# First cross layer: the opening row products of a half-unit's first tile move into the row block of the half-unit before

## The chip, the cores and the metric

One core of a Trainium2 chip runs the whole kernel. The metric is the device time in microseconds (us); the kernel before takes 131.48 us, the median of 3 runs (131.47 to 131.52).

## The reference, cut to what matters

Six cross layers on 4096 rows of 416 features, in bf16:

```python
B, F, D, L = 4096, 26, 16, 6          # Din = 416
def reference(x0, ws, bs):            # x0 (4096, 416), ws (6, 416, 416), bs (6, 416)
    x = x0
    for l in range(ws.shape[0]):
        x = x0 * (x @ ws[l] + bs[l]) + x
    return x
```

## The kernel before

**Layout.** The features lie on the partitions. 416 = 3 x 128 + 32: three blocks of 128 features (index m for outputs, k for inputs) and a remainder of 32. Columns are the 4096 batch rows: two units (s) of 2048 columns, each of four groups (g) of 512. `XM[i]` holds the three full blocks; `XR[i]` holds the remainder, with the four column groups of a unit stacked on partitions 0, 32, 64 and 96, so that one tile of 512 columns holds the remainder of a whole unit. `XRd` is a copy of the first remainder with its halves exchanged, so that group g also stands 64 partitions away. `WM`, `WR` and `WD` hold the weights: full rows, the 32 remainder rows repeated on all four partition groups, and a block form for the remainder's outputs.

**Products.** For an output block m, 512 columns get three full products (128 input rows each, L208 in the first layer, L173 in 32-column strips in the middle layers, L304 in the last) and one row product, which adds the 32 remainder rows. A row product uses only 32 rows of the array, at row group 0, 32, 64 or 96. Row products are at L226 in the first layer, at L179 (`mm_row`) in the middle layers and at L310 in the last. The remainder's outputs come from `mm_rem` (L185, L190).

**Behind the products.** `ew_main` takes a finished tile of 128 x 1024: ACT adds the bias and casts to bf16 (L159), DVE multiplies by x0 (L160) and adds x (L161). `ew_rem` does the same for the remainder (L165 to L167). All tiles that TensorE writes come from one pool, `psum`, of four buffers with one tag (`"ps"`); a tile waits until a buffer is free, that is until all that used the tile before it are done.

**First layer.** `first_layer(s)` runs once for each unit. It goes over two half-units h of two column groups each (gl = 0, 1). A half-unit takes three tiles `ph0` to `ph2`, one for each m, does 18 full products into them, and then one block of six row products in the order m = 0, 1, 2. The row group is `32 * ((2 * h + gl) ^ (2 if m == 1 else 0))`: for h = 0 it is 0, 32 (m = 0), 64, 96 (m = 1, from `XRd`), 0, 32 (m = 2); for h = 1 it is 64, 96, then 0, 32, then 64, 96. In h = 1 the tile `pr` follows, with `mm_rem` in its first half and, for s = 0, the transposes of unit 1's remainder (`x0_rem(1)`, L151) in its second half; DVE copies these into `XR[0]` and `XRd` (L154). For s = 0 and h = 0, `x0_rem(0)` does the same for unit 0 between the two column groups, with the tile `tpr` of its own.

**Middle layers and the end.** Layers 1 to 4 go over pairs of tiles (s, m); for the second tile of a pair the row products stand first and open the sums, right behind the first tile's row products: eight in a block. The last layer works with batch rows on the partitions, in four rounds, and stores the output.

**Order.** The instructions of each engine run in one fixed order. It follows the program's order in the main, but where an instruction's inputs come late, a later one that is ready may be laid ahead of it, on DVE above all.

Of the kernel before, what the change touches and what calls it, by code (L numbers as in the profile page):

```python
# [11 lines left out]
BF16 = mybir.dt.bfloat16  # L12
FP32 = mybir.dt.float32
# [3 lines left out]
def kernel(  # L17
# [7 lines left out]
    nc = tc.nc  # L25
    B, D = x0.shape
    L = ws.shape[0]
    P = 128
    NK = 3
# [4 lines left out]
    CW = 512  # L34
# [8 lines left out]
    psum = ctx.enter_context(tc.tile_pool(name="psum", bufs=4, space=bass.MemoryType.PSUM))  # L43
# [8 lines left out]
    WM = const.tile([P, L, NK, D], BF16)  # L52
    WR = const.tile([P, L, D], BF16)
# [10 lines left out]
    XRd = big.tile([P, NS * CW], BF16)  # L64
# [3 lines left out]
    def col0(s, g):  # L68
        return SW * s + CW * g
# [79 lines left out]
    def x0_rem(s, tpr):  # L149
        for i in range(4):  # L150
            nc.tensor.transpose(tpr[:, 128 * i:128 * i + 128], xrig[:, s, i, :], ident[:])  # L151
        for dst, src in ((slice(0, P), slice(0, P)), (slice(64, P), slice(0, 64)), (slice(0, 64), slice(64, P))):
            to = XR[0] if dst == src else XRd
            nc.vector.tensor_copy(to[dst, CW * s:CW * s + CW], tpr[src])  # L154

    def ew_main(l, s, m, h, pt, cur, nxt):
        c0 = col0(s, 2 * h)
        t = tpool.tile([P, 2 * CW], BF16, name="t")
        nc.scalar.activation(t[:], pt[:].rearrange("p a b -> p (a b)"), ACT.Identity, bias=bM[:, m, l:l + 1], scale=1.0)  # L159
        nc.vector.tensor_tensor(out=t[:], in0=t[:], in1=XM[0][:, m, c0:c0 + 2 * CW], op=ALU.mult)  # L160
        nc.vector.tensor_tensor(out=nxt[:, m, c0:c0 + 2 * CW], in0=t[:], in1=cur[:, m, c0:c0 + 2 * CW], op=ALU.add)  # L161

    def ew_rem(l, s, pr, curR, nxtR):
        tr = tpool.tile([P, 2 * CW], BF16, name="t")
        nc.scalar.activation(tr[:, 0:CW], pr, ACT.Identity, bias=bR[:, l:l + 1], scale=1.0)  # L165
        nc.vector.tensor_tensor(out=tr[:, 0:CW], in0=tr[:, 0:CW], in1=XR[0][:, CW * s:CW * s + CW], op=ALU.mult)  # L166
        nc.vector.tensor_tensor(out=nxtR[:, CW * s:CW * s + CW], in0=tr[:, 0:CW], in1=curR[:, CW * s:CW * s + CW], op=ALU.add)  # L167
# [15 lines left out]
    def mm_rem(l, s, pr, cur, curR):  # L183
        for g in range(NG):
            nc.tensor.matmul(pr[32 * g:32 * g + 32, :], lhsT=WD[:, l, g, :], rhs=curR[:, CW * s:CW * s + CW],  # L185
                             start=True, stop=False, tile_position=(0, 32 * g))
        for k in range(NK):
            for g in range(NG):
                c0 = col0(s, g)
                nc.tensor.matmul(pr[32 * g:32 * g + 32, :], lhsT=WM[:, l, k, NK * P:D], rhs=cur[:, k, c0:c0 + CW],  # L190
                      start=False, stop=(k == NK - 1), tile_position=(0, 32 * g))
# [7 lines left out]

    def first_layer(s):  # L200
        cur, curR, nxt, nxtR = XM[0], XR[0], XM[1], XR[1]
        for h in range(2):
            pt = [psum.tile([P, 2, CW], FP32, tag="ps", name=f"ph{m}") for m in range(NK)]

            def full(m, gl):
                c0 = col0(s, 2 * h + gl)
                for k in range(NK):
                    nc.tensor.matmul(pt[m][:, gl, :], lhsT=WM[:, 0, k, 128 * m:128 * m + 128], rhs=cur[:, k, c0:c0 + CW],  # L208
                                     start=(k == 0), stop=False)

            if s == 0 and h == 0:
                for gl in range(2):
                    for m in range(NK):
                        full(m, gl)
                    if gl == 0:
                        tp0 = psum.tile([P, CW], BF16, tag="ps", name="tpr")
                        x0_rem(0, tp0[:])
            else:
                for m in range(NK):
                    for gl in range(2):  # L220
                        full(m, gl)
            for m in range(NK):
                for gl in range(2):
                    rg = 32 * ((2 * h + gl) ^ (2 if m == 1 else 0))
                    src = XRd if m == 1 else curR
                    nc.tensor.matmul(pt[m][:, gl, :], lhsT=WR[rg:rg + 32, 0, 128 * m:128 * m + 128],  # L226
                                     rhs=src[rg:rg + 32, CW * s:CW * s + CW],
                                     start=False, stop=True, tile_position=(rg, 0))
            if h == 1:
                pr = psum.tile([P, 2, CW], FP32, tag="ps", name="pr")  # L230
                mm_rem(0, s, pr[:, 0, :], cur, curR)
                if s == 0:
                    x0_rem(1, pr[:, 1, :].bitcast(BF16)[:, 0:CW])
            for m in range(NK):
                ew_main(0, s, m, h, pt[m], cur, nxt)
            if h == 1:
                ew_rem(0, s, pr[:, 0, :], curR, nxtR)

    bias_setup()
    pe_filler(1, CW)  # L240
    for s in range(NS):
        first_layer(s)
# [15 lines left out]
    cur, curR = XM[1], XR[1]  # L258
    for l in range(1, LL):
        nxt, nxtR = XM[1 + (l % 2)], XR[1 + (l % 2)]  # L260
# [29 lines left out]
        cur, curR = nxt, nxtR  # L290
# [99 lines left out]
```

## Time and profile before

| | |
|---|---|
| median of 3 runs | 131.48 us (131.47 to 131.52) |
| profiled execution | 131.97 us |
| its span | 130.1 us |
| PE busy | 124.2 us (95%) |
| DVE busy | 107.5 us (83%) |
| ACT busy | 85.8 us (66%) |
| granted TensorE clock | 0.999 |

The span runs from the first to the last instruction of the profiled execution; 1.87 us lie around it. PE is TensorE's matmuls and PEld its weight loads, which overlap the matmuls. DVE is VectorE, ACT ScalarE. The chain is the work that ended last, followed back from the last instruction. Names such as L226 are lines of the kernel before.

### The profile page before, as it was taken

The numbers are of one execution on the slowest core, as the hardware profiler recorded it, in microseconds if no ns is written. First come the engines' busy times: TensorE is split into PE (matmuls) and PEld (weight loads), VectorE is DVE, ScalarE is ACT, GpSimd is POOL, SyncE is SP. The second block draws the span as 40 slices with busy tenths as digits, with TensorE's granted clock in tenths as the row PEclk, the third lists the DMA queues.
The fourth block names the chain that finished last, engine by engine and source line by source line (L and its number), as shares of the span: only waits on it lengthen the run. The fifth ranks groups of instructions, "written<-read, shape, count | busy, mean of one in ns | idle before, by whom it ended". The sixth has DMA issues, their size and how long they took to land.

```text
span 130.1 us, 3968 instructions
## 1 busy us (share of the span) xinstructions
PE 124.2 (95%) x1688; PEld 55.2 (42%) x1690; DVE 107.5 (83%) x197; ACT 85.8 (66%) x97; POOL 5.8 (4%) x17
## 2 busy tenths in 40 slices
PE   6999999999999999999999999999999999999960
PEld 2343343444444444545444434444445445445420
DVE  1012989999998898999898989898989899898991
ACT  0044594788849485849486849577848896569670
POOL 4002110610000000000000000000000000000000
PEclk9999999999999999999999999999999999999999
DMA  3999999999990000000000000000197999995754
GB/s 102 211 219 225 149 198 242 243 327 333 333 306 12 5 0 3 5 0 5 0 5 0 5 0 5 0 0 5 30 176 162 121 220 180 195 306 191 234 170 132
DMA packets 42185, 16.45 MB, mean 126 GB/s; under 512 B 30894, under 2 KB 42168, under 8 KB 42168
## 3 DMA queue, kind: packets, MB, share of 16 engines
q1 hardware_dynamic: 39368, 15.53, 54.4%
q10 hardware_dynamic: 2800, 0.67, 2.8%
q8 instruction: 13, 0.21, 0.7%
q14 instruction: 4, 0.03, 0.1%
HBM read 6.23 MB, written 3.41 MB: 74 GB/s over the span
## 4 chain that ended last, share of the span: by engine, by line
PE 89%; DVE 6%; issue 2%; ACT 1%; DVEq 0%
PE pt L173 49%; PE ph L208 13%; PE py L304 8%; PE pt L179 5%; PE pr L190 5%; DVE t L332 3%; PE wps L135 3%; DVE o L321 2%; PE pr L185 2%; PE ph L226 2%; PE py L310 1%; PE py L313 1%; ACT t L331 1%; PE tpr L151 0%; PE pr L151 0%
## 5 line engine op out<-in xcount | busy, mean ns | idle before, releaser
L173 PE MATMUL pt<-XM,WM 128*32 128x512 bf16 x1152 | 65.2, 379 | 0.0
L159 ACT ACTIVATE t<-pt,bM 128x1024 bf16<-128x1024 f32 x48 | 49.6, 1115 | 17.6 <-PE pt L179 17.6
L160 DVE TENSOR_TENSOR t<-t,XM 128x1024 bf16<-128x1024 bf16 x60 | 41.3, 690 | 6.0 <-ACT t L159 6.0
L161 DVE TENSOR_TENSOR XM<-t,XM 128x1024 bf16<-128x1024 bf16 x60 | 41.7, 696 | 3.4
L173 PEld LDWEIGHTS <-WM 128*32 128x32 bf16 x1152 | 29.8, 97 | 33.9 <-issue 5.4
L331 ACT CAST t<-py 128x416 bf16<-128x416 f32 (+1 forms) x23 | 14.8, 642 | 4.8 <-PE py L304 2.6
L304 PE MATMUL py<-WM,XM 128*128 128x416 bf16 x96 | 17.7, 340 | 0.0
L159 ACT ACTIVATE t<-ph,bM 128x1024 bf16<-128x1024 f32 x12 | 12.5, 1112 | 7.5 <-PE ph L226 7.5
L208 PE MATMUL ph<-XM,WM 128*128 128x512 bf16 x70 | 16.9, 387 | 0.2
L304 PEld LDWEIGHTS <-XM 128*128 128x128 bf16 x96 | 9.0, 98 | 8.5 <-issue 1.4
L332 DVE TENSOR_TENSOR t<-t,X0rows 128x416 bf16<-128x416 bf16 (+1 forms) x23 | 10.4, 456 | 1.2 <-ACT t L331 1.2
L208 PEld LDWEIGHTS <-WM 128*128 128x128 bf16 x72 | 6.9, 99 | 8.9 <-issue 1.9
L321 DVE TENSOR_TENSOR o<-t,XLrows 128x416 bf16<-128x416 bf16 (+1 forms) x23 | 10.4, 455 | 0.0
L165 ACT ACTIVATE t<-pr,bR 128x512 bf16<-128x512 f32 x10 | 6.4, 685 | 3.0 <-PE pr L190 2.1
L190 PE MATMUL pr<-XM,WM 128*32 128x512 bf16 x120 | 8.2, 379 | 0.0
L179 PE MATMUL pt<-XR,WR 32*128 32x512 bf16 x96 | 7.3, 379 | 0.0
L106 ACT ACT_TABLE_LOAD x1 | 1.3, 1283 | 6.6 <-DMA XM<-in_x_dram 6.6
L135 PE MATMUL wps<-warm 128*128 128x512 bf16 (+1 forms) x11 | 4.4, 593 | 1.2 <-DVE warm L94 1.2
L167 DVE TENSOR_TENSOR XR<-t,XR 128x512 bf16<-128x512 bf16 x10 | 4.2, 425 | 0.7
L190 PEld LDWEIGHTS <-WM 128*32 128x32 bf16 x120 | 3.2, 97 | 3.0
L166 DVE TENSOR_TENSOR t<-t,XR 128x512 bf16<-128x512 bf16 x10 | 4.2, 418 | 0.0
L125 POOL COPY WD<-WR 32x32 bf16<-32x32 bf16 (+1 forms) x8 | 3.4, 424 | 16.6 <-DMA WR<-in_ws_dram 16.3
(37 smaller groups left out, 29.7 us busy)
## 6 DMA issues: line engine op xcount, KB each, us to landing
X0rows<-in_x_dram SPq DMA_DIRECT2D x4, 832.0 KB, 11.6
out_dram<-o SPq DMA_DIRECT2D x9, 208.0 KB, 2.5
WM<-in_ws_dram SPq DMA_DIRECT2D x5, 312.0 KB
out_dram<-o SPq DMA_DIRECT2D x13, 104.0 KB, 1.8
WR<-in_ws_dram SPq DMA_DIRECT2D x4, 130.0 KB, 4.1
WM<-in_ws_dram ACTq DMA_DIRECT2D x1, 312.0 KB
XM<-in_x_dram SPq DMA_TRANSPOSE x8, 5.8
xrig<-in_x_dram ACTq DMA_DIRECT2D x4, 32.0 KB, 4.5
```

What stands on the lines that cost most here:

```text
L135: nc.tensor.matmul(wps[:, 0:cols], lhsT=warm[:, 0:P], rhs=warm[:, 0:cols], start=True, stop=True)
L159: nc.scalar.activation(t[:], pt[:].rearrange("p a b -> p (a b)"), ACT.Identity, bias=bM[:, m, l:l + 1], scale=1.0)
L160: nc.vector.tensor_tensor(out=t[:], in0=t[:], in1=XM[0][:, m, c0:c0 + 2 * CW], op=ALU.mult)
L161: nc.vector.tensor_tensor(out=nxt[:, m, c0:c0 + 2 * CW], in0=t[:], in1=cur[:, m, c0:c0 + 2 * CW], op=ALU.add)
L173: nc.tensor.matmul(pts[g // 2][32 * q:32 * q + 32, g % 2, :], lhsT=WM[:, l, k, 128 * m + 32 * q:128 * m + 32 * q + 32], rhs=cur[:, k, c0:c ...
L179: nc.tensor.matmul(pts[g // 2][:, g % 2, :], lhsT=WR[32 * g:32 * g + 32, l, 128 * m:128 * m + 128], rhs=curR[32 * g:32 * g + 32, CW * s:CW ...
L190: nc.tensor.matmul(pr[32 * g:32 * g + 32, :], lhsT=WM[:, l, k, NK * P:D], rhs=cur[:, k, c0:c0 + CW], start=False, stop=(k == NK - 1), tile ...
L208: nc.tensor.matmul(pt[m][:, gl, :], lhsT=WM[:, 0, k, 128 * m:128 * m + 128], rhs=cur[:, k, c0:c0 + CW], start=(k == 0), stop=False)
L304: nc.tensor.matmul(py[:, 0:D], lhsT=cur[:, k, q_cols(q, g)], rhs=WM[:, l, k, :], start=((not closes) and k == 0), stop=(closes and k == NK ...
L321: tc.keep_in_program_order(nc.vector.tensor_tensor(out=o, in0=t, in1=xl, op=ALU.add))
L331: nc.scalar.copy(tv, src)
L332: tc.keep_in_program_order(nc.vector.tensor_tensor(out=tv, in0=tv, in1=X0rows[:, b, :], op=ALU.mult))
```

## The change

In both units, the two row products of h = 1's tile `ph0` (m = 0) move from the end of h = 1 into the row block of h = 0 and open that tile's sum. The block of h = 0 now holds eight row products, in the order `ph0` of h = 0, `ph0` of h = 1, m = 2, m = 1 (row groups 0, 32, 64, 96, 0, 32, 64, 96). The block at the end of h = 1 holds four (m = 1 and m = 2; row groups 0, 32, 64, 96). h = 1's `ph0` is closed by its last full product (`stop`), and it takes its buffer ahead of h = 0's row block.

```diff
-        for h in range(2):
-            pt = [psum.tile([P, 2, CW], FP32, tag="ps", name=f"ph{m}") for m in range(NK)]
...
+        def full(pt, m, h, gl, after_row):
+            c0 = col0(s, 2 * h + gl)
+            for k in range(NK):
+                nc.tensor.matmul(pt[:, gl, :], lhsT=WM[:, 0, k, 128 * m:128 * m + 128], rhs=cur[:, k, c0:c0 + CW],
+                                 start=(k == 0 and not after_row), stop=(k == NK - 1 and after_row))
+
+        def row(pt, m, h, opens):
+            for gl in range(2):
+                rg = 32 * ((2 * h + gl) ^ (2 if m == 1 else 0))
+                src = XRd if m == 1 else curR
+                nc.tensor.matmul(pt[:, gl, :], lhsT=WR[rg:rg + 32, 0, 128 * m:128 * m + 128],
+                                 rhs=src[rg:rg + 32, CW * s:CW * s + CW],
+                                 start=opens, stop=not opens, tile_position=(rg, 0))
+
+        def ph(m):
+            return psum.tile([P, 2, CW], FP32, tag="ps", name=f"ph{m}")
+
+        pa = [ph(m) for m in range(NK)]
...
+        pb = [ph(0)]
+        row(pa[0], 0, 0, False)
+        row(pb[0], 0, 1, True)
+        row(pa[2], 2, 0, False)
+        row(pa[1], 1, 0, False)
+        for m in range(NK):
+            ew_main(0, s, m, 0, pa[m], cur, nxt)
+        for m in range(NK):
+            if m:
+                pb.append(ph(m))
+            for gl in range(2):
+                full(pb[m], m, 1, gl, m == 0)
+        row(pb[1], 1, 1, False)
+        row(pb[2], 2, 1, False)
+        pr = psum.tile([P, 2, CW], FP32, tag="ps", name="pr")
+        mm_rem(0, s, pr[:, 0, :], cur, curR)
+        if s == 0:
+            x0_rem(1, pr[:, 1, :].bitcast(BF16)[:, 0:CW])
+        for m in range(NK):
+            ew_main(0, s, m, 1, pb[m], cur, nxt)
+        ew_rem(0, s, pr[:, 0, :], curR, nxtR)
```

More of the change, by code (lines that the diff above doesn't have):

```diff
@@ L201, in first_layer @@
         cur, curR, nxt, nxtR = XM[0], XR[0], XM[1], XR[1]
-        for h in range(2):
-            pt = [psum.tile([P, 2, CW], FP32, tag="ps", name=f"ph{m}") for m in range(NK)]
[L205 to L221, printed above, removed]
+        def full(pt, m, h, gl, after_row):
[3 more added lines that the diff above has]
+                                 start=(k == 0 and not after_row), stop=(k == NK - 1 and after_row))
@@ L222, in first_layer @@
+        pa = [ph(m) for m in range(NK)]
+        if s == 0:
+            for m in range(NK):
+                full(pa[m], m, 0, 0, False)
+            tp0 = psum.tile([P, CW], BF16, tag="ps", name="tpr")
+            x0_rem(0, tp0[:])
+            for m in range(NK):
+                full(pa[m], m, 0, 1, False)
+        else:
             for m in range(NK):
                 for gl in range(2):
-                    rg = 32 * ((2 * h + gl) ^ (2 if m == 1 else 0))
-                    src = XRd if m == 1 else curR
@@ L226, in first_layer @@
[L226 to L237, printed above, removed]
+                    full(pa[m], m, 0, gl, False)
+        pb = [ph(0)]
[5 more added lines that the diff above has]
+            ew_main(0, s, m, 0, pa[m], cur, nxt)
+        for m in range(NK):
+            if m:
+                pb.append(ph(m))
+            for gl in range(2):
+                full(pb[m], m, 1, gl, m == 0)
@@ L239 @@
+        row(pb[1], 1, 1, False)
+        row(pb[2], 2, 1, False)
+        pr = psum.tile([P, 2, CW], FP32, tag="ps", name="pr")
+        mm_rem(0, s, pr[:, 0, :], cur, curR)
+        if s == 0:
+            x0_rem(1, pr[:, 1, :].bitcast(BF16)[:, 0:CW])
+        for m in range(NK):
+            ew_main(0, s, m, 1, pb[m], cur, nxt)
+        ew_rem(0, s, pr[:, 0, :], curR, nxtR)
     bias_setup()
```

## The prediction

> **What bounds the kernel now.** I read the page's busy shares first, then what each engine waited for, then the chain of work that ended last, in order of time, and last the timelines of DVE and ACT around the first layer.
>
> The page's first part, its chain by engine, and the one line of the waits that has the matmul queue as the waiting engine:
>
> ```profile
> PE 124.2 (95%) x1688; PEld 55.2 (42%) x1690; DVE 107.5 (83%) x197; ACT 85.8 (66%) x97; POOL 5.8 (4%) x17
> ...
> PE 89%; DVE 6%; issue 2%; ACT 1%; DVEq 0%
> ...
> PE wps L135 <- DVE warm L94: 1.2, 1, 1.2
> ```
>
> PE is busy 95% of the span, carries 89% of the chain, and waits once, 1.2 us, before its first instruction. From 1.19 to 116.84 us the chain is PE alone, but for scraps of "issue" of at most 0.05 us. So PE time that is taken out of the first layer should come out of the end, unless it turns into a wait.
>
> The chain in order of time (start, length, what), around the four blocks of row products (L226) and two rows from later:
>
> ```profile
> 11.21 0.60 PE ph L226 x6
> ...
> 15.99 0.54 PE ph L226 x6
> 16.53 0.33 PE pr L185 x4
> 16.86 0.65 PE pr L190 x12
> 17.51 0.33 PE pr L151 x4
> ...
> 21.72 0.54 PE ph L226 x6
> 22.26 3.99 PE ph L208 x18
> 26.25 0.54 PE ph L226 x6
> ...
> 30.55 0.54 PE pt L179 x8
> 31.09 2.70 PE pt L173 x48
> 33.80 0.22 PE pr L185 x4
> ...
> 106.07 0.29 PE py L310 x4
> 106.36 0.18 PE py L313 x4
> ```
>
> To be seen: six row products of the first layer take 0.54 us, and eight of the same shape in layer 1 (L179) take 0.54 us as well. Row products go by slots in which four row groups (0, 32, 64, 96) run side by side. Six products fill one slot and half of a second; the change is about that half.
>
> **A slot and its surroundings.** L190's twelve products are three slots of four and take 0.65 us: 0.65 / 3 = 0.217 us a slot. Two slots are 0.43, so a block's 0.54 holds 0.11 for entering the row form. A lone slot behind such an entry: 0.217 + 0.11 = 0.32 us. The nearest row with one is L310, 0.29 us at 416 columns where the next slot (L313) takes 0.18: again 0.11 for the entry. The form that comes next pays its own switch: L185 takes 0.33 us behind row products (16.53) and 0.22 behind column products (33.80). These switches stay: there are four blocks in row form before and after.
>
> **The change, part by part.** A unit is s (2048 columns), a half-unit is h.
>
> 1. Block at the end of h=0: six row products become eight (ph0 of h=0 with groups 0 and 32, ph0 of h=1 with 64 and 96; then m=2 with 0 and 32, m=1 with 64 and 96). By L179, which has the same sequence of groups and also lets rows open one tile (`first=True` for the second tile), 0.54 us: 0.00. Bounds: the block at 11.21 took 0.60, so an untidy one costs 0.06 more; below nothing is excluded for a block that holds more products. The two added weight loads lie beside the matmuls, as L179's eight do.
> 2. Block at the end of h=1: six products become four, one slot: 0.54 - 0.32 = 0.22 us saved, for each of two units. Bounds: nothing saved if the lone slot drains badly, and 0.54 - 0.28 = 0.26.
> 3. The 18 full products of the second half-unit's tiles, 3.99 us, keep their order; ph0's rows only stand ahead of its full products instead of behind. 0.00.
> 4. ACT: h=1's first tile is now complete with its own full products, about 13.1 us, and not with the block at 15.99. ACT is idle from 14.75 to 16.36, so that tile's ACTIVATE can run at 14.75 to 15.87. DVE gets it 1.6 us earlier, and its wait of 0.36 us at 17.14 can close. No gain for the end by itself, as PE doesn't wait for them.
> 5. Buffers: `psum` has four. ph0 of h=1 is now taken before h=0's block rather than behind it. In unit 0 the fourth buffer is that of `tpr`, released by the copies into XRd (9.61 + 0.88 = 10.49), which the m=1 row products at 11.21 waited for anyway: 0.00. In unit 1 it is a new wait, the first rival below.
> 6. Data that arrive at fixed times: PE reaches unit 1 0.22 us earlier and layer 1 0.43 us earlier. The last transposed loads of x0 are issued by 18.3 us, DMA traffic falls to 9 GB/s in 19.5 to 20.0, and their first use is at 22.9: over 2 us to spare. `xrig` for unit 1 is copied by 16.59 and used at 17.44. Layer 1's weights are issued at 18.35, right behind; at the 163 to 358 GB/s of 20.0 to 21.5 their 312 KB have passed by about 21.3, against a use at 27.3. No new wait.
>
> Sum: 2 x 0.22 = 0.43 us off PE, from 16.3 us on. Behind it PE is the chain to 116.84, and the tail (ACT L331, DVE L332, L321, the stores) hangs on PE's last round, so it moves with it. Span 130.1 becomes 129.67. The profiled execution took 131.97, 1.87 around its span and 0.49 above the median of the runs, 131.48; I take the difference off the median: 131.48 - 0.43 = **131.05 us**.
>
> The Trainium skill, "TensorE: Matmul & The Clock Gate", section "Measured speedup vs the span model", gives 3.07 times for four row tiles; an estimate from it, read as a price per product, has six products cost three quarters of eight, and then moving two of them saves nothing. The trace has 0.54 us for six and for eight, which speaks against that reading; it is kept as the third rival.
>
> **Rivals.**
>
> *First: the fourth buffer of unit 1 comes too late (slower than before).* The buffers of unit 0's h=1 come free in the order ph0, ph1, ph2, pr; unit 1's three tiles take the first three, and ph0 of unit 1's h=1 takes pr's. Before, that was wanted at 22.19; now at 21.66 - 0.22 = 21.44, by the second pair of products in the block, with the other row products and everything behind them queued on PE. pr is released by L165 on ACT, which waited for the copies out of pr's other half on DVE:
>
> ```profile
> 20.38 0.69 ACT L165 ACTIVATE t<-pr,bR 128x512 bf16<-128x512 f32 x1 [0.89 <-DVE XRd L154]
> ...
> 17.50 0.69 DVE L160 TENSOR_TENSOR t<-t,XM 128x1024 bf16<-128x1024 bf16 x1 [0.36 <-ACT t L159]
> 18.23 0.69 DVE L161 TENSOR_TENSOR XM<-t,XM 128x1024 bf16<-128x1024 bf16 x1
> 18.95 0.42 DVE L154 COPY XR<-pr 128x512 bf16<-128x512 bf16 x1
> 19.41 0.88 DVE L154 COPY XRd<-pr 64x512 bf16<-64x512 bf16 x2
> 20.20 1.28 DVE L160 TENSOR_TENSOR t<-t,XM 128x1024 bf16<-128x1024 bf16 x2
> ```
>
> It ends at 21.07, 0.37 us ahead of the new need. It matters where the copies stand in DVE's fixed order: here behind ph0's multiply and add, ahead of ph1's. If they stay there, with ph0's pair now starting at 17.14 as DVE comes free, they end about 19.85 and pr is free at 20.6: no wait, 0.8 us to spare. But the order was laid out by what was ready when; ph0's pair is now ready 1.6 us earlier, and ph1's may slip in ahead of the copies. A pair takes 1.34 us (12.78 to 14.12): ph0 to 18.5, ph1 to 19.85, copies to 21.2, L165 to 21.97, 0.06 for the signal: PE waits 0.59 us, and -0.43 + 0.59 = +0.16: 131.64. It turns slower than before once pr is released after 21.87, that is copies ending after about 21.1. With ph2's multiply ahead too, 0.67 more: 132.3; if only ph1's multiply slips in, the release is at about 21.3 and nothing is lost. For it: DVE's order already interleaves tiles (two L160 in a row at 20.20). Against: the transposes end at 17.84 less 0.22, ahead of 18.5, and the copies stand earlier in the program than ph1's pair.
>
> The Trainium skill, "TensorEngine Tiling (Array Packing)", section "Gotcha 1: PSUM Pressure", says that row tiling increases the pressure on PSUM and that different row tiles write different banks; this is the same mechanism in general words, and the margin of 0.37 us above is its size here.
>
> *Second: only one unit gains.* If pr is late by some 0.2 us, or the order laid out for PE puts unit 1's early row products behind the other six (three slots in that block, 0.22 lost), half of the gain stays: 131.48 - 0.22 = 131.26. For it: the fourth buffer is the last free in both units. Against: in the whole trace PE's row products stand in program order.
>
> *Third: the block of eight costs three slots, or cost goes per product.* Then 0.22 is lost at each block of eight and gained at each block of four: 131.48. Against: L179 in twelve places, each 0.54.
>
> **How the numbers follow.** Chances: forecast 0.62, first rival 0.17 (0.09 of it near 131.64, 0.08 beyond), second 0.13, third 0.04; another order further on that costs or brings some tenths 0.04, split evenly. What a measurement of this kernel can tell from no change is about 0.2%, 0.26 us: 131.22 to 131.74. Faster: 0.62 + 0.02, and a little of the second where the wait is short: 0.66. Within: 0.09 + 0.12 + 0.04, less that little: 0.24. Slower: 0.08 + 0.02 = 0.10. The range goes down to the wider bound of step 2 (0.26 twice, 130.96, less 0.06 for reading) and up past the first rival at one pair: 130.9 to 131.7. The forecast's own range is 130.9 to 131.2.
>
> **What would show it.** Right: four row blocks of 8, 4, 8, 4 products at 0.54 to 0.60, 0.32, 0.54, 0.32 us in the chain; L173's first product at 27.35 and not 27.78; an ACTIVATE of ph0 at about 14.75; L165 before 21.4 and no PE wait at the block of unit 1; PE's last round 0.43 us earlier. Wrong: a gap on PE at about 21.5 released by ACT L165; row products of unit 1 spread over three slots; an equal PE saving with the end unmoved, which would mean that the tail isn't tied to PE.

## The result and the profile after

The changed kernel takes 131.26 us, the median of 19 runs, against 131.48 us before (19 runs): a ratio of 0.9984, 95% interval 0.9978 to 0.9990, or 0.13 to 0.29 us less. That lies between the forecast (131.05) and no change, and by chance on the figure of the second rival. The profile shows that neither the forecast nor the second rival happened: the first rival did, at nearly the price given for it (0.62 us of PE time against 0.59), and two gains that the prediction had not seen paid it back: 0.20 us where layer 1 begins, and 0.18 us at the end of the program, whose cause no run here shows.

Two executions at a granted clock of 0.757 and 0.664, one of an experiment below and one of the kernel before, took 163.02 and 185.72 us and are left out.

Two lines of the page after, then, of the waits that have the matmul queue as the waiting engine, the new one that tells (two more, of 0.2 us each and for loads, end before the first row block):

```profile
PE 123.4 (95%) x1690; PEld 55.1 (42%) x1690; DVE 107.5 (83%) x197; ACT 85.7 (66%) x97; POOL 6.1 (5%) x17
...
PE 73%; DVE 11%; DMA 8%; issue 3%; ACT 2%; DVEq 0%; ACTq 0%
```

```profile
PE ph L213 <- ACT t L165: 0.2, 1, 0.2
```

PE's share of the chain falls from 89% to 73%, and a wait for ACT's L165, the instruction that releases `pr`, has appeared at the row products (L213 is now their line, L206 that of the full products). The chain from 11.47 to 21.77 us no longer runs on PE but on ACT and DVE. That is about half of the fall; the 8% of DMA are two loads ahead of the first row block, through which the chain passes from 0.74 to 11.00 us.

PE's timeline of the kernel after, the row blocks and what stands behind them (start, busy time, instruction):

```profile
11.04 0.60 PE L213 MATMUL ph<-XR,WR 32*128 32x512 bf16 x6
11.28 0.38 PE L213 MATMUL ph<-XRd,WR 32*128 32x512 bf16 x2
11.59 0.82 PE L206 MATMUL ph<-XM,WM 128*128 128x512 bf16 x3
...
15.67 0.39 PE L213 MATMUL ph<-XRd,WR 32*128 32x512 bf16 x2
15.67 0.39 PE L213 MATMUL ph<-XR,WR 32*128 32x512 bf16 x2
15.99 0.40 PE L185 MATMUL pr<-XR,WD 128*32 128x512 bf16 x4
...
21.19 0.39 PE L213 MATMUL ph<-XR,WR 32*128 32x512 bf16 x2
21.82 0.40 PE L213 MATMUL ph<-XR,WR 32*128 32x512 bf16 x4 [0.24 <-ACT t L165]
22.03 0.39 PE L213 MATMUL ph<-XRd,WR 32*128 32x512 bf16 x2
22.35 0.82 PE L206 MATMUL ph<-XM,WM 128*128 128x512 bf16 x3
...
26.34 0.39 PE L213 MATMUL ph<-XRd,WR 32*128 32x512 bf16 x2
...
26.67 0.40 PE L185 MATMUL pr<-XR,WD 128*32 128x512 bf16 x4
26.89 0.82 PE L190 MATMUL pr<-XM,WM 128*32 128x512 bf16 x12
27.54 0.82 PE L173 MATMUL pt<-XM,WM 128*32 128x512 bf16 x12
```

From start to start: eight products in unit 0 take 0.55 us (11.04 to 11.59), four take 0.32 and 0.33 (15.67 to 15.99 and 26.34 to 26.67), as forecast. Unit 1's block of eight takes 1.16 us (21.19 to 22.35): behind its first two products it stands still until 21.82. A block without the wait takes 0.54, so 0.62 is lost.

DVE's and ACT's timelines after, in the same stretch:

```profile
16.01 0.98 DVE L161 TENSOR_TENSOR XM<-t,XM 128x1024 bf16<-128x1024 bf16 x1
16.91 0.68 DVE L160 TENSOR_TENSOR t<-t,XM 128x1024 bf16<-128x1024 bf16 x1
17.62 0.69 DVE L161 TENSOR_TENSOR XM<-t,XM 128x1024 bf16<-128x1024 bf16 x1
18.23 0.68 DVE L160 TENSOR_TENSOR t<-t,XM 128x1024 bf16<-128x1024 bf16 x1
18.95 0.69 DVE L161 TENSOR_TENSOR XM<-t,XM 128x1024 bf16<-128x1024 bf16 x1
19.67 0.42 DVE L154 COPY XR<-pr 128x512 bf16<-128x512 bf16 x1
20.12 0.86 DVE L154 COPY XRd<-pr 64x512 bf16<-64x512 bf16 x2
...
21.08 0.69 ACT L165 ACTIVATE t<-pr,bR 128x512 bf16<-128x512 f32 x1 [2.86 <-DVE XRd L154]
```

Before, one pair of multiply and add stood between the wait for ph0 and the copies; now two do (16.91 and 18.23). The copies end at 20.98, L165 at 21.77, and only then is the fourth buffer free for PE.

The prediction read the start of layer 1 from the chain, "27.76 0.01 issue", and saw no wait there. PE's timeline before, and ACT's, show one:

```profile
26.72 0.40 PE L185 MATMUL pr<-XR,WD 128*32 128x512 bf16 x4
26.94 0.82 PE L190 MATMUL pr<-XM,WM 128*32 128x512 bf16 x12
27.78 2.77 PE L173 MATMUL pt<-XM,WM 128*32 128x512 bf16 x48
...
26.61 2.12 ACT L159 ACTIVATE t<-ph,bM 128x1024 bf16<-128x1024 f32 x2 [1.40 <-PE ph L226]
```

L190's twelve products hold PE for three slots, 0.65 us, so L173 could begin at 27.59; it began at 27.78, 0.06 behind the end of ph0's ACTIVATE at 27.72. After, it begins at 26.89 + 0.65 = 27.54, as ph0 of unit 1 is complete long before. The chain did not show this because it counts a matmul until its end: one takes 0.38 us and the next begins 0.217 behind it, so some 0.16 us of waiting lie under the last matmul. Starts show it.

Added up behind the second row block (T1: 15.93 before, 15.67 after) the profiles give -0.21 for unit 0's four products, +0.62 for the stall, -0.21 for unit 1's four and -0.20 at layer 1: about zero, and L173 begins 11.85 us behind T1 before and 11.87 after. Yet the timed runs are 0.22 faster. Most of that lies at the end of the program. The last store is issued 99.64 us behind L173's first product before and 99.63 after, but the span goes on for another 2.73 us before and 2.56 after (the traces' spans are 130.15 and 129.73 us). Among SyncE's waits on the program's last line, those for PE's queue differ (in all, times, longest; the first two lines are of before, the last two of after):

```profile
127.42 0.37 ACTq L322 DMA_DIRECT2D out_dram<-o  x1
SPq L385 <- PEq L385: 0.8, 2, 0.6
...
127.17 0.37 ACTq L337 DMA_DIRECT2D out_dram<-o  x1
SPq L400 <- PEq L400: 0.6, 2, 0.4
```

The change moves nothing there, and why this end is shorter stays open. It does mean that the timed gain needs no shorter stall than the profile's. How long the stall is varies from execution to execution, as the experiments show.

### The profile page after: what moved, and what is told of

Read it like the earlier page. It is cut to its first block, busy times and chain, and to the rows that moved or that the text cites. A ratio compares the mean times of both kernels' runs of the same rounds, so it can differ in the third digit from the quotient of the medians.

```text
span 129.7 us, 3968 instructions
## 1 busy us (share of the span) xinstructions
PE 123.4 (95%) x1690; PEld 55.1 (42%) x1690; DVE 107.5 (83%) x197; ACT 85.7 (66%) x97; POOL 6.1 (5%) x17
## 4 chain that ended last, share of the span: by engine, by line
PE 73%; DVE 11%; DMA 8%; issue 3%; ACT 2%; DVEq 0%; ACTq 0%
PE pt L173 49%; PE py L319 8%; PE pt L179 5%; PE pr L190 4%; DMA WR<-in_ws_dram 4%; DMA XM<-in_x_dram 4%; DVE t L347 3%; PE ph L206 3%; DVE t L160 2%; DVE XM L161 2%; DVE o L336 2%; PE pr L185 2%; PE ph L213 1%; PE py L325 1%; ACT t L159 1%
## 5 line engine op out<-in xcount | busy, mean ns | idle before, releaser
L173 PE MATMUL pt<-XM,WM 128*32 128x512 bf16 x1152 | 65.2, 379 | 0.0
L173 PEld LDWEIGHTS <-WM 128*32 128x32 bf16 x1152 | 29.7, 97 | 33.8 <-issue 5.1
L206 PE MATMUL ph<-XM,WM 128*128 128x512 bf16 x72 | 16.5, 379 | 0.2 <-DMA XM<-in_x_dram 0.2
L206 PEld LDWEIGHTS <-WM 128*128 128x128 bf16 x72 | 6.8, 98 | 8.6 <-issue 1.2
L165 ACT ACTIVATE t<-pr,bR 128x512 bf16<-128x512 f32 x10 | 6.4, 684 | 5.0 <-DVE XRd L154 2.9
L190 PE MATMUL pr<-XM,WM 128*32 128x512 bf16 x120 | 8.2, 379 | 0.0
L167 DVE TENSOR_TENSOR XR<-t,XR 128x512 bf16<-128x512 bf16 x10 | 4.2, 424 | 0.7
L190 PEld LDWEIGHTS <-WM 128*32 128x32 bf16 x120 | 3.2, 97 | 3.0
```

Of the source, the lines that this page charges most:

```text
L173: nc.tensor.matmul(pts[g // 2][32 * q:32 * q + 32, g % 2, :], lhsT=WM[:, l, k, 128 * m + 32 * q:128 * m + 32 * q + 32], rhs=cur[:, k, c0:c ...
L206: nc.tensor.matmul(pt[:, gl, :], lhsT=WM[:, 0, k, 128 * m:128 * m + 128], rhs=cur[:, k, c0:c0 + CW], start=(k == 0 and not after_row), sto ...
```

## Experiments

Theory A: a saved slot is worth 0.22 us a unit; the fourth buffer of unit 1 costs 0.4 to 0.6; a wait of 0.2 at layer 1's start is gone. Theory B: slots, less a shorter wait for the buffer, and no hidden wait. Neither theory knew of the shorter end of the program. Each kernel is compared with the kernel before, run on the same chip.

**The change in one unit only.** `first_layer_old` is the function of the kernel before.

```diff
     for s in range(NS):
-        first_layer(s)
+        (first_layer if s == 0 else first_layer_old)(s)   # unit 0 only; s == 1 for unit 1 only
```

> The change in unit 0 only; unit 1 keeps its two blocks of six. Theory A: each unit that is changed saves one slot of 0.22 us on PE; what the change lost is a wait of some 0.6 us in unit 1's first row block (the fourth buffer, released by L165 behind DVE's copies), and it won 0.2 us more where unit 1's change lets layer 1's first tile find a free buffer (before, L173 began at 27.78 behind ph0's ACTIVATE, 26.61 + 1.11 = 27.72, and not at 27.58). Here there is neither that wait nor that gain: 131.48 - 0.22 = 131.26, no PE gap at 21.4, L173 still beginning 1.07 us after L185's first product. Rival B: no hidden wait at layer 1's start; the change is two slots (0.43) less a wait that is only some 0.2 in the timed runs. Then also 131.26. This run alone tests that one unit's slot is worth 0.22.

> The change in unit 1 only. DVE's copies stand behind ph0's pair as before, so pr is released at about 21.1 and unit 1's block at 21.66 does not wait. Theory A: one slot (0.22) and the hidden wait at layer 1's start (0.2) are saved: 131.06, L173 beginning 0.87 us after L185's first product. Rival B: one slot only: 131.26.

Unit 0 only: 131.17 us, ratio 0.9976 (0.9967 to 0.9985), 0.20 to 0.43 less. Unit 1 only: 131.18, ratio 0.9971 (0.9960 to 0.9982), 0.24 to 0.53 less. By the medians each half of the change brings at least as much by itself as both together, so the two disturb each other. In the profile of unit 0 only, the full products behind unit 1's block begin 0.57 behind the block's start (0.53 before), and L173 begins 1.06 behind L185; in that of unit 1 only, 0.87, as theory A has it. The two times are too near each other to tell A from B, and A's difference of 0.2 between them did not come: unit 0 only has the shorter end of the program and unit 1 only has not (the table below).

**The copies back behind ph0's pair.**

```diff
-            nc.vector.tensor_copy(to[dst, CW * s:CW * s + CW], tpr[src])
+            cp = nc.vector.tensor_copy(to[dst, CW * s:CW * s + CW], tpr[src])
+            if s == 1:
+                tc.keep_in_program_order(cp)
...
+        if (l, s, h, m) == (0, 0, 1, 1):
+            tc.keep_in_program_order(mul)      # mul: ew_main's multiply
...
+        ew_main(0, s, 0, 1, pb[0], cur, nxt)   # now ahead of x0_rem(1)
         if s == 0:
             x0_rem(1, pr[:, 1, :].bitcast(BF16)[:, 0:CW])
-        for m in range(NK):
+        for m in range(1, NK):
```

> The whole change, and DVE's copies for unit 1 pinned between ph0's pair and ph1's pair of unit 0's second half-unit, as they stood before. Theory A: no wait in unit 1's block (pr free by about 20.5), so two slots and the hidden wait: 131.48 - 0.43 - 0.2 = 130.85. Rival B: two slots: 131.05. Both expect the gap on PE at 21.4 to be gone; if it stays, the buffer of pr was not its cause.

130.88 us, ratio 0.9948 (0.9935 to 0.9961), 0.51 to 0.85 less: A's figure, and B's 0.43 lies outside. PE's and DVE's timelines of this kernel:

```profile
21.14 0.60 PE L217 MATMUL ph<-XR,WR 32*128 32x512 bf16 x6
21.37 0.38 PE L217 MATMUL ph<-XRd,WR 32*128 32x512 bf16 x2
21.68 4.06 PE L210 MATMUL ph<-XM,WM 128*128 128x512 bf16 x18
...
17.45 0.69 DVE L165 TENSOR_TENSOR XM<-t,XM 128x1024 bf16<-128x1024 bf16 x1
18.17 0.42 DVE L154 COPY XR<-pr 128x512 bf16<-128x512 bf16 x1
18.63 0.86 DVE L154 COPY XRd<-pr 64x512 bf16<-64x512 bf16 x2
...
16.92 0.22 PEld L151 LDWEIGHTS <-xrig 128*128 128x128 bf16 x4 [0.51 <-POOL xrig L128]
```

Unit 1's block takes 0.54 us and the gap is gone, so it hung on the place of the copies. The last line is a wait that comes next: the transposes now wait for POOL's copy into `xrig` and begin 1.07 behind L185 in place of 0.98.

**The copies one pair later still**, the copies pinned as above:

```diff
+        for m in range(NK):
+            ew_main(0, s, m, 1, pb[m], cur, nxt)
         if s == 0:
             x0_rem(1, pr[:, 1, :].bitcast(BF16)[:, 0:CW])
-        for m in range(NK):
-            ew_main(0, s, m, 1, pb[m], cur, nxt)
```

> The changed kernel with DVE's copies for unit 1 pinned one pair later, behind ph2's multiply and add. Theory A: pr is released one pair (1.34 us) later and PE waits that much more: 131.26 + 1.34 = 132.60, with a gap of about 1.8 us on PE in unit 1's block. Rival (the wait is for another thing): 131.26, or a smaller loss where only XRd is late.

> The same kernel as e8_copies_last, for a profile at full clock. Theory A: the block of unit 1 stands still about 0.5 + 1.34 = 1.8 us behind its first two products, released by ACT L167; time about 132.6. Rival: no such gap.

The first measurement gave 132.70 us, the median of three executions that spread from 132.50 to 134.42; the second 132.59 us, ratio 1.0079 (1.0064 to 1.0095). PE's timeline of the second:

```profile
21.27 0.39 PE L215 MATMUL ph<-XR,WR 32*128 32x512 bf16 x2
22.94 0.40 PE L215 MATMUL ph<-XR,WR 32*128 32x512 bf16 x4 [1.28 <-ACT t L167]
...
23.48 4.06 PE L208 MATMUL ph<-XM,WM 128*128 128x512 bf16 x18
```

One pair more on DVE costs 132.59 - 131.26 = 1.33 us, a pair's length. In the profiles the release, counted from the first row block's start, is 1.32 later (L167 ends 12.05 behind it, L165 in the changed kernel 10.73), while the block loses 1.67 and not 0.62, 1.05 more, since PE reaches it 0.28 later. With this and the run above, the place of the copies in DVE's order sets the stall.

**A slot of filler where layer 1 begins**, in the kernel before and in the kernel after:

```diff
+                else:
+                    for g in range(NG):
+                        nc.tensor.matmul(pr[32 * g:32 * g + 32, 1, :], lhsT=WD[:, 0, g, :], rhs=curR[:, CW * s:CW * s + CW],
+                                         start=True, stop=True, tile_position=(0, 32 * g))
```

> The kernel before with four more column products (one slot of 0.22 us, the shape of L185) behind unit 1's remainder products, into the half of pr that nothing reads; the result is unchanged. Theory A: PE waits there for ph0's buffer anyway, so the slot costs almost nothing: 131.48 to 131.52. Rival B: PE is never idle there, so it costs 0.22: 131.70.

> The changed kernel with the same extra slot of four column products behind unit 1's remainder products (the result is unchanged). Theory A: the change took away the wait for ph0's buffer at layer 1's start, so nothing hides the slot any more: 131.26 + 0.22 = 131.48, L173 beginning 0.87 + 0.22 us after L185's first product. Rival B (never a wait there): the slot costs 0.22 here as well, but then it should have cost it in the kernel before too, where it cost 0.04. Rival C: the wait is still there in the changed kernel: 131.26 to 131.30.

Before plus filler: 131.53, ratio 1.0000 (0.9992 to 1.0009). After plus filler: 131.44, ratio 0.9995 (0.9986 to 1.0004), 0.18 more than after, and 0.14 more than the changed kernel measured beside it (131.30, below). So the slot costs nothing that shows in the kernel before and most of its price after the change. The starts say it more sharply: the filler moves L173 from 1.06 to 1.09 behind L185 in the kernel before, and from 0.87 to 1.09 in the kernel after. A wait stood there, and the change has taken it away. PE's timeline of before plus filler shows it filled in, with no time left over:

```profile
26.57 0.82 PE L190 MATMUL pr<-XM,WM 128*32 128x512 bf16 x12
27.21 0.39 PE L236 MATMUL pr<-XR,WD 128*32 128x512 bf16 x4
27.43 1.04 PE L173 MATMUL pt<-XM,WM 128*32 128x512 bf16 x16
```

**The opening products last in the block** (order m = 0, m = 1, m = 2, then ph0 of h = 1):

```diff
         row(pa[0], 0, 0, False)
-        row(pb[0], 0, 1, True)
-        row(pa[2], 2, 0, False)
         row(pa[1], 1, 0, False)
+        row(pa[2], 2, 0, False)
+        row(pb[0], 0, 1, True)
```

> The changed kernel with the row block of eight in the order m = 0, m = 1, m = 2, and the opening products of the second half-unit's first tile last. DVE's copies still stand behind ph1's pair. Theory A: still two slots, but the fourth buffer is wanted one slot (0.22) later, and six of the products no longer queue behind it: the stall falls by 0.22 to some 0.25, 131.04 to 131.12. Rival: the stall comes from something else than the fourth buffer (the late copies into XR and XRd themselves, say): no change, 131.26.

130.92 us, ratio 0.9950 (0.9936 to 0.9964). More than expected: 0.65 less by the medians, 0.47 to 0.84 by the interval of the ratio, with 0.36 to 0.44 forecast. PE's timeline:

```profile
21.06 0.39 PE L213 MATMUL ph<-XR,WR 32*128 32x512 bf16 x2
21.07 0.39 PE L213 MATMUL ph<-XRd,WR 32*128 32x512 bf16 x2
21.29 0.53 PE L213 MATMUL ph<-XR,WR 32*128 32x512 bf16 x4
21.75 4.06 PE L206 MATMUL ph<-XM,WM 128*128 128x512 bf16 x18
```

The block takes 0.69 us here, 0.15 more than a block without a wait, though the copies still stand behind two pairs on DVE. Six products no longer queue behind the wait, and the fourth buffer is wanted a slot later. The products that read XR and XRd start at once, at 21.06 and 21.07, so the copies' own data are not what the stall waits for; the buffer that L165 releases is. By the profile that makes -0.45 up to L173, and the end of the program is 0.19 shorter than before, as in the changed kernel: -0.64 together.

**How long the stall is.** The changed kernel again, and one with POOL's copy into `xrig` moved to ACT, with DVE's copies pinned where the changed kernel has them:

```diff
-    nc.gpsimd.tensor_copy(xrig[:, 1].rearrange("p i (g r) -> p i g r", g=NG), xrem[:].rearrange("p (g i) r -> p i g r", g=NG))
...
+        ew_main(0, s, 0, 1, pb[0], cur, nxt)
+        if s == 0:
+            tc.keep_in_program_order(nc.scalar.copy(xrig[:, 1].rearrange("p i (g r) -> p i g r", g=NG),
+                                                    xrem[:].rearrange("p (g i) r -> p i g r", g=NG)))
+        ew_main(0, s, 1, 1, pb[1], cur, nxt)
         if s == 0:
             x0_rem(1, pr[:, 1, :].bitcast(BF16)[:, 0:CW])
```

> The changed kernel once more, for a second profile. Theory A in its corrected form: the stall in unit 1's block is (T0 + 10.78) - (T1 + 5.52), with T0 the start of the first row block, from which ACT and DVE run without a break to the release of pr, and T1 the start of the second, which waits for a transposed load of x0. Its first profile had T1 - T0 = 4.63 and lost 0.63; the other five profiles have 4.72 to 4.79, which makes 0.47 to 0.54. So here T1 - T0 near 4.78, a loss near 0.48, and 131.48 - 0.43 - 0.20 + 0.48 = 131.33, measured before as 131.26. Rival: the loss is 0.6 whatever T1 - T0 is.

> The changed kernel with the copy into xrig for unit 1 moved from POOL to ACT, behind ph0's ACTIVATE; DVE's copies still stand behind ph1's pair. In the profiles the DVE add that runs beside POOL's copy takes 0.98 to 1.13 us and its like elsewhere 0.69. Theory A: without POOL's copy it takes 0.69, pr is released about 0.3 us earlier, and the stall in unit 1 falls by as much: 131.28 - 0.3 = 130.98, with a gap of 0.1 to 0.3 us left. Rival (the late add has no part in the stall): 131.28.

The repetition: 131.30 us, ratio 0.9981 (0.9972 to 0.9990). T1 - T0 was 4.77, yet the block lost 0.63 (21.06 to 22.23), not 0.48: the formula missed. DVE's add beside POOL's copy took 1.13 us in that execution and 0.98 in the after-plus-filler one, whose block lost 0.48. Without POOL's copy: 131.09, ratio 0.9965 (0.9953 to 0.9978). DVE's and PE's timelines:

```profile
15.65 0.69 DVE L162 TENSOR_TENSOR XM<-t,XM 128x1024 bf16<-128x1024 bf16 x1
...
20.98 0.60 PE L214 MATMUL ph<-XR,WR 32*128 32x512 bf16 x6
21.39 0.39 PE L214 MATMUL ph<-XRd,WR 32*128 32x512 bf16 x2
21.72 4.06 PE L207 MATMUL ph<-XM,WM 128*128 128x512 bf16 x18
```

The add takes 0.69, the block 0.74, so 0.20 is lost in place of 0.48 to 0.63. Which instruction pays varies: with the copies back behind ph0's pair, and with the opening products last, the add took 0.69 and the multiply beside POOL's copy 1.10. The Trainium skill, "SBUF — State Buffer", section "Who interferes with whom", says that a DVE instruction with two inputs in SBUF contends with a GpSimd instruction that reads SBUF; the add here is of that kind, and 0.98 to 1.13 beside the copy against 0.69 without it agrees.

**The kernel before again.**

> The kernel before once more, for a second profile. Its first one began the second row block (T1) at 15.93; six of the seven profiles with the same first part have 15.51 to 15.67. Theory A: here T1 near 15.54 and L173 from T1 + 11.85 = 27.39; before and after differ little behind T1 in the profiles that lost 0.6 in the block, and by some 0.2 in the one that lost 0.47.

131.69 us in its one execution. T1 was 15.66 and L173 began at 27.51, again 11.85 behind it. So the first profile of before began its second block 0.27 us late, and the distance from there on is the kernel's own. T1 lies between 15.46 and 16.00 in the twelve profiles at full clock, and its place is not the change's doing: unit 0's block of eight costs what the block of six did.

**All twelve profiles behind T1.** The first column is the distance from T1 to L173's first product, where slots, stall and hidden wait show. The second is from there to the end of the span. The third is their sum less the mean of the two profiles of before, the fourth the timed median less that of before on the same chip (us).

| kernel | T1 to L173 | L173 to end | profile | timed |
|---|---|---|---|---|
| before, first and again | 11.85, 11.85 | 102.37, 102.39 | 0 | 0 |
| after, first and again | 11.87, 11.88 | 102.19, 102.20 | -0.17, -0.15 | -0.22, -0.27 |
| unit 0 only | 11.66 | 102.18 | -0.39 | -0.32 |
| unit 1 only | 11.46 | 102.38 | -0.39 | -0.31 |
| copies back | 11.33 | 102.38 | -0.52 | -0.61 |
| copies later | 13.05 | 102.19 | +1.01 | +1.10 |
| before plus filler | 11.88 | 102.36 | +0.01 | +0.04 |
| after plus filler | 11.94 | 102.18 | -0.11 | -0.13 |
| opening last | 11.40 | 102.19 | -0.64 | -0.65 |
| `xrig` on ACT | 11.45 | 102.40 | -0.38 | -0.40 |

The first column follows theory A (copies back carries 0.09 for the wait for `xrig`). The second has two values, 102.36 to 102.40 and 102.18 to 102.20, and each kernel that was profiled twice has the same one both times; the shorter one goes with the shorter wait for PE's queue on the program's last line. Which kernel gets which is not explained by anything shown here. With both columns the profiles come within 0.12 us of the timed runs.

## Why the prediction was right or wrong

**Slots: right.** Blocks of eight, four, eight and four were forecast at 0.54, 0.32, 0.54 and 0.32 us; 0.55, 0.32 and 0.33 were measured for the first, second and fourth, and 0.54 for the third where nothing waits. The sum of 0.43 for two units stands. The third rival is refuted: four products take 0.32 and eight 0.54. The reading of the Trainium skill's 3.07 ("TensorE: Matmul & The Clock Gate", "Measured speedup vs the span model") as a price per product makes the saving zero, and these rows refute it too.

**The fourth buffer: the mechanism was priced, and given the wrong chance.** The first rival had everything but the likelihood: the buffer of pr, wanted at 21.44, the copies done at 21.2 and L165 at 21.97, a wait of 0.59. In the profile the buffer was wanted at 21.19, the copies end at 20.98, L165 at 21.77, and the block loses 0.62, where the sum had put nothing. The sign of being wrong that the prediction named, a gap on PE at about 21.5 released by ACT L165, is what came. The rival got 0.17, since the copies stand earlier in the program and their input would be there in time by before's trace. What follows when was laid out ahead of the run, though, and need not have the trace's times: before's trace already had ph0's add (18.23) ahead of copies whose input was ready at 17.84. That sign was in the lines shown, and was not weighed.

**The step that failed for the sum: the start of layer 1.** The prediction's step 4 says of h=1's first tile, complete earlier: "No gain for the end by itself, as PE doesn't wait for them." That step works with unit 0's times, but the tile of unit 1 is the one that layer 1 follows. There PE did wait, 0.20 us, for ph0's buffer, and the earlier completion of unit 1's ph0 is just what removes the wait. The fillers show both sides of that.

**A step that failed unseen: the end.** The sum lets the tail "move with" PE's last round. Up to the last store it did (99.64 and 99.63 us behind L173), but the end of the program came 0.18 us sooner than that. This stays open.

**So 131.26 is misses that cancel:** -0.43 for slots, -0.20 at layer 1 and +0.62 for the stall leave about nothing, and in the profiles the gain is the 0.18 at the end, which has nothing to do with the argument as far as is known. That the time fell between the forecast and no change is luck; the range reached up to 131.7 because the first rival was priced. The forecast of 131.05 would have been 130.85 with the hidden wait seen and the copies in place, and 130.88 was measured for that kernel.

**Data that arrive at fixed times: right in the end, but close.** None of the waits named there appeared with the change alone. With the stall gone, `xrig` did become a wait (0.09 us), though the prediction's two numbers, 16.59 and 17.44, leave 0.85 us to spare, or 0.63 with PE 0.22 earlier; in that execution POOL's copy began at 15.73 and took 1.14 us beside DVE.

**A better version.** With the copies pinned the kernel takes 130.88 us, with the opening products last 130.92: both beat the kernel before and, by 0.34 us or more, the changed one.

## What to carry to other kernels

When a tile is opened earlier, ask which buffer it takes and what the slowest reader of that buffer is; then put the instruction that can wait last in its block, so that nothing queues behind it. Work that becomes ready earlier is laid out anew on the engines that consume it, and may be set ahead of the one thing that someone is waiting for: pin it. And look for waits on a pipelined engine in the starts of its instructions, not in a chain made of their ends: here 0.2 us lay under the last matmul's tail.

## What was not expected of the hardware

A DVE instruction on two 128x1024 bf16 tiles took 0.98 to 1.13 us beside the POOL copy into `xrig` (the add in nine profiles, the multiply in two) and 0.69 without it. From the last store's issue to the end of the span it took about 2.74 us in some kernels and 2.56 in others, the same in both profiles of each kernel that was profiled twice. And with matmuls of 0.38 us that begin every 0.217 us, a wait of 0.2 us leaves a gap of only about 0.01 in the chain: PE looked busy throughout.
